# Raw weight bits loaded from ScalarE's queue, chunk outputs queued a step later, the cosine's rounding constant added by ScalarE

## The chip, the cores and the metric

The kernel runs on one core of a Trainium2 chip. The metric is the device time in microseconds of one execution, as the median of three runs. One execution before the change was also recorded by the hardware profiler; all rows below come from that execution.

## The reference, cut to what matters

Three stages follow each other: a linear attention with a norm, a mixture of eight experts with one expert per token, and a dense layer with h * cos(h) between its two products.

```python
kv  = np.einsum('bhsd,bhse->bhde', k, v)            # 8 batches, 8 heads, 576 tokens, 64 wide
out = np.einsum('bhsd,bhde->bhse', q, kv)
x   = out / rms(out) * g_norm                       # -> 4608 tokens x 512

expert_idx = np.argmax(logits(x), axis=1)           # 8 experts, 512 -> 1024 -> 512
y = gate_w * (np.maximum(x @ w1[e], 0) @ w2[e])     # for each token's expert e

h = y @ w_in                                        # 512 -> 2048, w_in is float64
return (h * np.cos(h)) @ w_out                      # 2048 -> 512, w_out is float64
```

## The kernel before, in words

The instructions of each engine run in the order in which the program writes them down, and each engine starts its own instructions and DMAs in that order. An instruction that has to wait for another engine or for a transfer holds up all that stands behind it on its engine. Three engines issue DMAs: SP (`nc.sync`), ACT (`nc.scalar`) and POOL (`nc.gpsimd`), each into its own queue.

**The expert stage** (in the profile some 190 to 720 us) works on 16 chunks of 304 gathered tokens. A loop over `g` runs 130 steps. Step g does for hidden slice f of chunk c the first product (`layer1`, L241 on PE, then the two evictions L247 on ACT and L248 on DVE), and for the slice two steps back the second product (`layer2`, L258). `load_piece` loads the weights of a slice into one of four `raw` tiles by two DMAs on SP (L130, L134), three steps before `split_piece` turns them into high and low parts on ACT (L141) and DVE (L142). `turn_x` transposes the next chunk's tokens (L224, L229, L230) and `gate_x` works out the gate of the next chunk (L182 on POOL to L208 on DVE), writes it to DRAM and reads it back as a broadcast (L212, L216 on SP). When a chunk's last slice is done, `store_y` (L263 to L269) writes the chunk's token list and four output tiles by five DMAs on SP.

**The conversion** of the last layer's float64 weights to float32 is spread over the same steps. The generator `conv` is advanced once or twice at the end of each step. There are 32 conversions: 16 of `w_in` (layer 0), 16 of `w_out` (layer 1). Each loads 512 KB of raw bits into one of two `c_raw` tiles (`convert_load`, `raw_bits`, L283 and L288 on SP), and runs `bits`: an absolute value on ACT into `c_mk` (L297), a multiply and add on POOL (L298), and four integer passes on DVE (L299, L301, L303, L305), with a pause of the generator after the first three. After every second conversion of layer 0, `prepare` adds and splits the blocks and issues seven DMAs of 256 KB on SP (`ws`, L416); a conversion of layer 1 issues one (`wc`, L328). So two conversions of layer 0 take 13 turns of the generator, one of layer 1 takes 4. The load of conversion x + 1 is issued at the start of conversion x: for an even x that is 4 turns ahead of its use, and right behind the seven DMAs of `prepare`; for an odd x it is 9 turns ahead.

**The last stage** (some 720 to 1526 us) runs 72 steps, `step(i)`, eight for each block of 512 tokens. In a step PE makes seven products for h (L1150, 42 matmuls) and then the out-product of step i - 2 (L1243, 24 matmuls). DVE puts the seven products together into two tiles h (L1166). `turns` then forms u = h / (2 pi) on ACT (L1134) and r = u rounded to a whole number on POOL (L1135), by adding and taking away the constant `ROUND` = 1.5 * 2^23. In the next step DVE takes u - r (L1192), ACT the absolute value and the sine (L1170, L1174), DVE multiplies with h (L1175), and ACT and DVE split the result into high and low (`high` L1180, `low` L1184). The tiles u and r have two buffers for the two tiles of a step, so r is written again only after `low` of the step before has read it. Behind `turns`, in steps 1 to 7, `second_split` splits the second weights (L343 on ACT, L344 on DVE), and in the steps in which the next block's tokens are prepared, `tokens_of` does subtractions and splits (L371, L343, L344).

Of the kernel before, what the change touches and what calls it, by code (L numbers as in the profile page):

```python
# [10 lines left out]
F32 = mybir.dt.float32  # L11
F32R = mybir.dt.float32r
I32 = mybir.dt.int32
ACTF = mybir.ActivationFunctionType
ALU = mybir.AluOpType
# [14 lines left out]
CH = 304  # L30
# [6 lines left out]
def tile_kernel(ctx, tc, q, k, v, g_norm, emb, tau, w1, w2, w_in, w_out, out):  # L37
    nc = tc.nc
# [7 lines left out]
    yT = dram.tile([DM, NT + CH], F32, name="yT")  # L46
# [3 lines left out]
    perm = dram.tile([NT + CH], I32, name="perm")  # L50
# [27 lines left out]
    chunks = []  # L78
    for vi, (e, idx) in enumerate(VISITS):
        for i in idx:  # L80
            chunks.append(dict(
                row=(lambda e=e: e * NT + reg(itab[0:1, 0, e:e + 1], CH, mybir.EngineType.Pool)) if i else (lambda e=e: e * NT),
                col=lambda e=e, i=i: reg(itab[0:1, 1 + i, e:e + 1], NT),
# [8 lines left out]
    LAG = 2  # L92
    NC = len(chunks)
# [50 lines left out]
    V = nc.vector  # L144
    P = SimpleNamespace()
# [115 lines left out]
                )  # L261

    def store_y(c):  # L263
        col = c["col"]()
        nc.sync.dma_start(out=perm[bass.ds(col, CH)].rearrange("(p r) -> p r", r=4), in_=c["rows"])
        for d in range(4):
            o = P.yo.tile([128, CH], F32, name="yo", tag="yo")
            V.tensor_tensor(out=o, in0=c["y"][d][:, 0:CH], in1=c["gate"], op=ALU.mult)
            nc.sync.dma_start(out=yT[d * 128:(d + 1) * 128, bass.ds(col, CH)], in_=o)  # L269


    w_in32, w_out32 = w_in.bitcast(I32), w_out.bitcast(I32)
# [5 lines left out]
    CONV = [(0, m) for m in range(DF2 // 128)] + [(1, m) for m in range(DF2 // 128)]  # L278

    def raw_bits(raw, layer, m):  # L280
        rv = raw.rearrange("p c x -> p (c x)")
        if layer == 0:
            nc.sync.dma_start(  # L283
                out=rv.rearrange("p (k c) -> p k c", k=4),
                in_=w_in32[:, m * 256:(m + 1) * 256].rearrange("(k p) c -> p k c", p=128),
            )
        else:
            nc.sync.dma_start(out=rv, in_=w_out32[m * 128:(m + 1) * 128, :])  # L288

    def convert_load(x):  # L290
        cv[x] = P.cv.tile([128, 512, 2], I32, name="c_raw", tag="c_raw", bufs=2)
        raw_bits(cv[x], *CONV[x])

    def bits(raw, t, mk, out):
        lo, hi = raw[:, :, 0], raw[:, :, 1]
        hf = hi.bitcast(F32)
        nc.scalar.activation(out=mk, in_=hf, func=ACTF.Abs)  # L297
        nc.gpsimd.tensor_scalar(out=mk, in0=mk, scalar1=-1.0, scalar2=TINY, op0=ALU.mult, op1=ALU.add)  # L298
        V.tensor_scalar(out=t, in0=hi, scalar1=3, scalar2=0x3FFFFFF8, op0=ALU.logical_shift_left, op1=ALU.bitwise_and)  # L299
        yield  # L300
        V.scalar_tensor_tensor(out=t, in0=lo, scalar=29, in1=t, op0=ALU.logical_shift_right, op1=ALU.bitwise_or)  # L301
        yield
        V.scalar_tensor_tensor(out=t, in0=hi, scalar=-0x40000000, in1=t, op0=ALU.bitwise_and, op1=ALU.bitwise_or)  # L303
        yield
        V.scalar_tensor_tensor(  # L305
            out=out, in0=mk.bitcast(I32), scalar=31, in1=t, op0=ALU.arith_shift_right, op1=ALU.bitwise_and
        )

    def convert(x):
        layer, m = CONV[x]  # L310
        if x == 0:
            convert_load(0)
            yield
        raw = cv.pop(x)
        if x + 1 < len(CONV):
            convert_load(x + 1)
        t = P.cv.tile([128, 512], I32, name="c_t", tag="c_t", bufs=2)
        mk = P.cv.tile([128, 512], F32, name="c_mk", tag="c_mk", bufs=1)
        if layer == 0:
            if m % 2 == 0:  # L320
                cv["a"] = P.sc.tile([128, 1024], F32, name="sa", tag="sa")
            yield from bits(raw, t, mk, cv["a"][:, m % 2 * 512:m % 2 * 512 + 512].bitcast(I32))
            yield
            if m % 2:
                yield from prepare(m // 2, cv.pop("a"))
        else:
            yield from bits(raw, t, mk, t)
            nc.sync.dma_start(out=wc[m], in_=t.bitcast(F32))  # L328
            yield

# [173 lines left out]
    if True:  # L506
# [62 lines left out]
        for i in range(2):  # L569
# [7 lines left out]
            out=ident, in_=ones, pattern=[[1, 128]], compare_op=ALU.is_equal, fill=0.0, base=0, channel_multiplier=-1  # L577
# [322 lines left out]
        for t in range(NTILE):  # L900
            j, b, r = where(t)
# [61 lines left out]
    if True:  # L963
# [43 lines left out]
        for g in range(NC * 8 + LAG):  # L1007
            c, f = divmod(g, 8)
            if g == 8 * NC - 1:
                for _ in prep:  # L1010
                    pass
                nc.scalar.preload_act_table_set("trig_and_small")
            if c < NC:
                if f == 1 and 0 < c < NC - 2:
                    load_list(chunks[c + 2])
                if f == 3 and 0 < c < NC - 2:
                    load_x(chunks[c + 2])
                if f == {0: 0, 1: 2, 2: 0}.get(c):
                    prep = gate_x(chunks[c])
                if f == 7 and 2 <= c < NC - 1:  # L1020
                    for _ in prep:
                        pass
                    prep = gate_x(chunks[c + 1])
                layer1(chunks[c], f)
                if g <= OPEN and ranking:
                    cur["po"] = P.ps_x.tile([128, 512], F32, name="xp", tag="xp").rearrange("p (o x) -> p o x", o=1)
                    for it in ranking:
                        next(it)
                    ranking.clear()
            if c == 1:  # L1030

                for x in {5: (0,), 6: (1, 2), 7: (3,)}.get(f, ()):
                    turn_x(chunks[c + 1], x)
            if g >= LAG:
                c2, f2 = divmod(g - LAG, 8)
                layer2(chunks[c2], f2)
                if f2 == 7:
                    store_y(chunks[c2])
                    if c2 == NC - 2:
                        first["x"] = tokens_of(0, lambda: raw_of()[:, 0:512])  # L1040
            if "x" in first:
                next(first["x"], None)

            if g == 8 * NC - 4:
                assert next(conv, None) is None
                cvctx.close()
                WAB.append(ctx.enter_context(tc.tile_pool(name="wb", bufs=1)).tile([128, 7, 2, 256], F32R, name="wb"))
                weights_again(0)
                weights_again(1)
            if g < OPEN:  # L1050
                paused.clear()
                advance(8)
            splits = bool(late) and late[0][0] <= g
            if splits:
                split_piece(*late.pop(0)[1])
            if g == OPEN - 1:

                for d in range(4):
                    nc.sync.dma_start(out=yT[d * 128:(d + 1) * 128, CH:512], in_=none[:, 0:512 - CH].bitcast(F32))
            if g == OPEN:  # L1060
                assert not ranking
                while active:
                    paused.clear()
                    advance(1)
                after_placing()
                load_list(chunks[2])
                load_x(chunks[2])
            for p in when.get(g, ()):
                late.append((split_at[p], load_piece(p)))
                late.sort(key=lambda x: x[0])  # L1070
            if g >= OPEN:
                for _ in range(1 if splits and g % 3 else 2):
                    next(conv, None)
            if c < NC:
                next(prep, None)
                if c != 1 and c + 1 < NC and 3 <= f < 7:
                    turn_x(chunks[c + 1], f - 3)
# [7 lines left out]
    ROUND = 1.5 * 2.0 ** 23  # L1085
    if True:
# [45 lines left out]

        def turns(p, u, r):
            nc.scalar.activation(out=u, in_=p, func=ACTF.Copy, scale=1.0 / (2 * math.pi))  # L1134
            nc.gpsimd.tensor_scalar(out=r, in0=u, scalar1=ROUND, scalar2=-ROUND, op0=ALU.add, op1=ALU.add)  # L1135

        def times_cos(p, u, r, hi, lo):
            V.tensor_tensor(out=u, in0=u, in1=r, op=ALU.subtract)
            nc.scalar.activation(out=r, in_=u, func=ACTF.Abs)
            nc.scalar.activation(out=u, in_=r, func=ACTF.Sin, scale=-2 * math.pi, bias=half_pi)  # L1140
            V.tensor_tensor(out=r, in0=u, in1=p, op=ALU.mult)
            nc.scalar.activation(out=hi, in_=r, func=ACTF.Copy)
            V.tensor_tensor(out=lo, in0=r, in1=hi.bitcast(F32), op=ALU.subtract)
# [17 lines left out]
        def step(i):  # L1161
# [27 lines left out]
            if prev:  # L1189
                for m in range(2):  # L1190
                    h, u, r, g_ = prev[m]
                    V.tensor_tensor(out=u, in0=u, in1=r, op=ALU.subtract)  # L1192
                cos_a(0)
                cos_b(0)
            if stored is not None:
# [243 lines left out]
```

## Time and profile before

| what | value |
|---|---|
| median of three runs | 1528.04 us (1525.45 to 1530.85) |
| the profiled execution's own time | 1528.09 us |
| its span, first to last instruction | 1526.4 us |
| mean granted TensorE clock | 0.947 of full speed |
| busy in the span: PE, DVE, ACT, POOL | 92%, 70%, 51%, 41% |
| DMA queues of SP, POOL, ACT | 260.46, 19.66, 9.78 MB |

The span is 1.7 us shorter than the execution's own time, which includes what lies around the first and last instruction. Busy shares are means over stages with different limits; a stage is read by its own stretch of the span, and there by which wait ended last.

### The profile page before, as it was taken

The numbers are of one execution on the slowest core, as the hardware profiler recorded it, in microseconds if no ns is written. First come the engines' busy times: TensorE is split into PE (matmuls) and PEld (weight loads), VectorE is DVE, ScalarE is ACT, GpSimd is POOL, SyncE is SP. The second block draws the span as 40 slices with busy tenths as digits, with TensorE's granted clock in tenths as the row PEclk, the third lists the DMA queues.
The fourth block names the chain that finished last, engine by engine and source line by source line (L and its number), as shares of the span: only waits on it lengthen the run. The fifth ranks groups of instructions, "written<-read, shape, count | busy, mean of one in ns | idle before, by whom it ended". The sixth has DMA issues, their size and how long they took to land.

```text
span 1526.4 us, 26934 instructions
## 1 busy us (share of the span) xinstructions
PE 1398.2 (92%) x9545; PEld 1288.3 (84%) x9545; DVE 1066.7 (70%) x2201; ACT 771.0 (51%) x1503; POOL 627.0 (41%) x459
## 2 busy tenths in 40 slices
PE   8877587689889989999889999999999999999996
PEld 8766587679889989999778898988888888888895
DVE  2533865687778688884677777777787777778664
ACT  3534632345345344533555656565656555555553
POOL 0223444353435345540334544444443535354443
PEclk8868788899999999999999999999999999999999
DMA  9999828579667787855856666565665666565550
GB/s 266 258 185 198 241 57 196 147 168 249 190 169 222 206 225 211 201 123 165 279 181 192 215 194 199 181 216 186 201 198 188 207 190 204 169 225 175 178 160 30
DMA packets 223670, 291.71 MB, mean 191 GB/s; under 512 B 33148, under 2 KB 127008, under 8 KB 223528
## 3 DMA queue, kind: packets, MB, share of 16 engines
q1 hardware_dynamic: 202440, 260.46, 59.6%
q0 software_dynamic: 15808, 19.66, 4.8%
q10 hardware_dynamic: 5280, 9.78, 2.3%
q8 instruction: 78, 1.28, 0.4%
q14 instruction: 64, 0.52, 0.1%
HBM read 241.28 MB, written 48.49 MB: 190 GB/s over the span
## 4 chain that ended last, share of the span: by engine, by line
DVE 29%; PE 20%; ACT 20%; issue 10%; DMA 9%; POOL 7%; SPq 2%; another core or an unknown queue 1%; DVEq 0%; ACTq 0%; POOLq 0%
PE hps L241 7%; ACT u L1174 6%; PE y L258 6%; POOL r L1135 5%; ACT r L1170 5%; DVE h L1166 4%; DVE u L1192 4%; DVE one L1166 4%; DMA raw<-in_moe_w 3%; DMA c_raw<-in_moe_w_in 3%; DVE ring L344 2%; DVE g L1184 2%; DVE three L1166 2%; DVE sx L371 2%; PE o L1243 2%
## 5 line engine op out<-in xcount | busy, mean ns | idle before, releaser
L1135 POOL TENSOR_SCALAR r<-u 128x512 f32<-128x512 f32 x144 | 312.8, 2187 | 475.0 <-ACT u L1134 475.0
L1243 PE MATMUL o<-ring,g 128*128 128x512 f32 x1728 | 417.5, 396 | 4.5 <-ACT o_sb L1254 2.1
L1243 PEld LDWEIGHTS o<-ring,g 128*128 128x128 f32 x1728 | 318.8, 188 | 80.9 <-ACT o_sb L1254 4.8
L241 PE MATMUL hps<-xT,ring 128*128 128x304 f32 x1536 | 254.1, 316 | 15.3 <-DVE h L248 6.7
L258 PE MATMUL y<-h,ring 128*128 128x304 f32 x1536 | 242.1, 307 | 10.2 <-ACT ring L141 9.4
L241 PEld LDWEIGHTS hps<-xT,ring 128*128 128x128 f32 x1536 | 230.2, 197 | 18.9 <-DVE h L248 7.9
L258 PEld LDWEIGHTS y<-h,ring 128*128 128x128 f32 x1536 | 226.8, 193 | 11.3 <-ACT ring L141 9.6
L1192 DVE TENSOR_TENSOR u<-u,r 128x512 f32<-128x512 f32 x144 | 117.3, 817 | 104.0 <-POOL r L1135 104.0
L1170 ACT ACTIVATE r<-u 128x512 f32<-128x512 f32 x144 | 90.4, 628 | 190.8 <-DVE u L1192 190.7
L1175 DVE TENSOR_TENSOR r<-u,h 128x512 f32<-128x512 f32 x144 | 99.8, 693 | 53.1 <-ACT u L1174 53.1
L1134 ACT ACTIVATE u<-h 128x512 f32<-128x512 f32 x144 | 91.1, 633 | 81.5 <-DVE h L1166 73.8
L1150 PEld LDWEIGHTS p<-ring,wb 128*128 128x128 f32 x840 | 106.0, 195 | 10.0 <-DVE h L1166 8.6
L142 DVE TENSOR_TENSOR ring<-raw,ring 128x1024 fp32r<-128x1024 f32 x72 | 91.7, 1273 | 31.9 <-ACT ring L141 27.7
L1150 PE MATMUL p<-ring,wb 128*128 128x256 f32 x840 | 107.6, 289 | 6.4 <-DVE h L1166 6.4
L1150 PEld LDWEIGHTS p<-ring,wa 128*128 128x128 f32 x840 | 105.9, 195 | 8.2 <-DVE h L1166 6.7
L1150 PE MATMUL p<-ring,wa 128*128 128x256 f32 x840 | 107.1, 288 | 5.7 <-DVE h L1166 5.7
L247 ACT ACTIVATE h<-hps 128x304 fp32r<-128x304 f32 x128 | 53.4, 417 | 110.3 <-PE hps L241 97.9
L1174 ACT ACTIVATE u<-r,half_pi 128x512 f32<-128x512 f32 x144 | 104.3, 724 | 4.7
L182 POOL TENSOR_TENSOR gx<-xr,g_bc 76x512 f32<-76x512 f32 x64 | 101.7, 1621 | 7.5 <-ACT gx L191 7.5
L165 POOL DMA_INDIRECT xr<-xs,rows x64 | 88.1, 1377 | 39.9 <-issue 15.6
L298 POOL TENSOR_SCALAR c_mk<-c_mk 128x512 f32<-128x512 f32 x32 | 25.2, 788 | 186.1 <-ACT c_mk L297 165.3
L1184 DVE TENSOR_TENSOR g<-r,g 128x512 fp32r<-128x512 f32 x144 | 92.7, 684 | 0.2 <-ACT g L1180 0.2
(230 smaller groups left out, 2054.1 us busy)
## 6 DMA issues: line engine op xcount, KB each, us to landing
wa<-ws SPq DMA_DIRECT2D x252, 256.0 KB
wb<-ws SPq DMA_DIRECT2D x252, 256.0 KB
raw<-in_moe_w SPq DMA_DIRECT2D x144, 256.0 KB
ws<-wa SPq DMA_DIRECT2D x56, 256.0 KB
yT<-yo SPq DMA_DIRECT2D x64, 152.0 KB
xs<-xg ACTq DMA_DIRECT2D x12, 780.0 KB
km<-in_k SPq DMA_DIRECT2D x8, 1024.0 KB
vm<-in_v SPq DMA_DIRECT2D x8, 1024.0 KB
```

Source lines behind the costliest of these rows:

```text
L182: nc.gpsimd.tensor_tensor(out=gx[:, r].rearrange("p (h d) -> p h d", h=H), in0=t[:, r, 0:DM].rearrange("p (h d) -> p h d", h=H), in1=g_bc[ ...
L241: nc.tensor.matmul(out=p[:, 0:CH], lhsT=w[:, a, k * 128:(k + 1) * 128], rhs=c["xT"][b_][k], start=(n == 0), stop=(n == 11),)
L258: nc.tensor.matmul(out=c["y"][d][:, 0:CH], lhsT=w[:, a, 512 + d * 128:512 + (d + 1) * 128], rhs=h[b_], start=(f == 0 and i == 0), stop=(f ...
L1135: nc.gpsimd.tensor_scalar(out=r, in0=u, scalar1=ROUND, scalar2=-ROUND, op0=ALU.add, op1=ALU.add)
L1150: nc.tensor.matmul(out=out, lhsT=w[:, wi, a, k * 128:(k + 1) * 128], rhs=x[xi][:, b_, k * 256:(k + 1) * 256], start=(n == 0), stop=(n == 5),)
L1166: V.tensor_tensor(out=out, in0=x, in1=y, op=ALU.add)
L1170: nc.scalar.activation(out=r, in_=u, func=ACTF.Abs)
L1174: nc.scalar.activation(out=u, in_=r, func=ACTF.Sin, scale=-2 * math.pi, bias=half_pi)
L1175: V.tensor_tensor(out=r, in0=u, in1=h, op=ALU.mult)
L1184: V.tensor_tensor(out=g_[1], in0=r, in1=g_[0].bitcast(F32), op=ALU.subtract)
L1192: V.tensor_tensor(out=u, in0=u, in1=r, op=ALU.subtract)
L1243: nc.tensor.matmul(out=ob[b][t], lhsT=g_[a][:, t * 128:(t + 1) * 128], rhs=w[:, b_, m * 512:m * 512 + 512], start=(q_ == 0 and m == 0 and ...
```

## The change

Raw bits are now started from ACT's queue. Conversion x issues the load of conversion x + 2, into the tile that it has itself just read, one turn after its last DVE pass; the first two loads are issued together at the start, and the first conversion begins one turn later. The `wc` store moves to the turn after the last pass. `store_y` computes the four output tiles where it did, and its five DMAs are issued by `flush` at the end of the next step (for the last two chunks at once). In the last stage ACT makes r = h / (2 pi) + ROUND itself, and DVE takes ROUND off again in the subtraction, which becomes (r - ROUND) - u, of opposite sign; an absolute value follows.

```diff
     def store_y(c):
-        col = c["col"]()
-        nc.sync.dma_start(out=perm[bass.ds(col, CH)].rearrange("(p r) -> p r", r=4), in_=c["rows"])
+        o = [P.yo.tile([128, CH], F32, name="yo", tag="yo") for _ in range(4)]
         for d in range(4):
-            o = P.yo.tile([128, CH], F32, name="yo", tag="yo")
-            V.tensor_tensor(out=o, in0=c["y"][d][:, 0:CH], in1=c["gate"], op=ALU.mult)
-            nc.sync.dma_start(out=yT[d * 128:(d + 1) * 128, bass.ds(col, CH)], in_=o)
+            V.tensor_tensor(out=o[d], in0=c["y"][d][:, 0:CH], in1=c["gate"], op=ALU.mult)
+
+        def flush():
+            col = c["col"]()
+            nc.sync.dma_start(out=perm[bass.ds(col, CH)].rearrange("(p r) -> p r", r=4), in_=c["rows"])
+            for d in range(4):
+                nc.sync.dma_start(out=yT[d * 128:(d + 1) * 128, bass.ds(col, CH)], in_=o[d])
+
+        return flush
...
     def raw_bits(raw, layer, m):
-            nc.sync.dma_start(
+            nc.scalar.dma_start(
                 out=rv.rearrange("p (k c) -> p k c", k=4),
...
-            nc.sync.dma_start(out=rv, in_=w_out32[m * 128:(m + 1) * 128, :])
+            nc.scalar.dma_start(out=rv, in_=w_out32[m * 128:(m + 1) * 128, :])
...
     def convert(x):
         if x == 0:
             convert_load(0)
+            convert_load(1)
+            yield
             yield
         raw = cv.pop(x)
-        if x + 1 < len(CONV):
-            convert_load(x + 1)
...
             yield from bits(raw, t, mk, cv["a"][:, m % 2 * 512:m % 2 * 512 + 512].bitcast(I32))
             yield
+            convert_load(x + 2)
             if m % 2:
                 yield from prepare(m // 2, cv.pop("a"))
         else:
             yield from bits(raw, t, mk, t)
+            yield
             nc.sync.dma_start(out=wc[m], in_=t.bitcast(F32))
-            yield
+            if x + 2 < len(CONV):
+                convert_load(x + 2)
...
                 if f2 == 7:
-                    store_y(chunks[c2])
+                    flush = store_y(chunks[c2])
+                    if c2 >= NC - 2:
+                        flush()
...
                 for _ in range(1 if splits and g % 3 else 2):
                     next(conv, None)
+            if g >= LAG and f2 == 0 and 0 < c2 < NC - 1:
+                flush()
...
         def turns(p, u, r):
             nc.scalar.activation(out=u, in_=p, func=ACTF.Copy, scale=1.0 / (2 * math.pi))
-            nc.gpsimd.tensor_scalar(out=r, in0=u, scalar1=ROUND, scalar2=-ROUND, op0=ALU.add, op1=ALU.add)
+            nc.scalar.activation(out=r, in_=p, func=ACTF.Copy, scale=1.0 / (2 * math.pi), bias=ROUND)
+
+        def parts(u, r):
+            V.scalar_tensor_tensor(out=u, in0=r, scalar=-ROUND, in1=u, op0=ALU.add, op1=ALU.subtract)
 
         def times_cos(p, u, r, hi, lo):
-            V.tensor_tensor(out=u, in0=u, in1=r, op=ALU.subtract)
+            parts(u, r)
...
                 for m in range(2):
                     h, u, r, g_ = prev[m]
-                    V.tensor_tensor(out=u, in0=u, in1=r, op=ALU.subtract)
+                    parts(u, r)
```

## Rows read from the trace of the kernel before

**Rows 1.** Windows by stretch: length, busy us (instructions) by engine, PEclk, DMA share, GB/s.

```profile
290.00:540.00 250.00, 219.61 (x1545) 215.09 (x1544) 185.69 (x360) 111.68 (x246) 104.42 (x80) 0.96 0.77 212
540.00:700.00 160.00, 159.65 (x1171) 159.13 (x1170) 127.11 (x259) 72.26 (x166) 76.50 (x61) 0.99 0.69 174
...
740.00:816.00 76.00, 65.58 (x355) 57.06 (x354) 57.48 (x118) 43.90 (x74) 23.28 (x12) 0.91 0.62 193
816.00:1508.00 692.00, 687.75 (x4245) 611.28 (x4244) 515.82 (x930) 400.94 (x708) 318.42 (x162) 1.00 0.58 188
```

**Rows 2.** Waits of ACT, 290 to 540: waiter <- releaser, total us, times, longest.

```profile
ACT c_mk L297 <- DMA c_raw<-in_moe_w_in: 49.8, 7, 11.4
...
ACT ring L141 <- DMA raw<-in_moe_w: 10.6, 4, 5.8
```

**Rows 3.** Waits of SP's queue, 290 to 540.

```profile
SPq L269 <- DVE yo L268: 48.4, 12, 10.4
```

**Rows 4.** Timeline of PE: start, length, instruction [idle before <-releaser].

```profile
246.71 3.38 PE L258 MATMUL y<-h,ring 128*128 128x304 f32 x12 [9.43 <-ACT ring L141]
...
275.24 0.77 PE L224 MATMUL xp<-ident,xr 76*128 76x76 f32 x4 [7.96 <-DVE xT L230]
...
343.11 0.77 PE L224 MATMUL xp<-ident,xr 76*128 76x76 f32 x4 [4.61 <-DVE xT L230]
...
512.46 3.38 PE L241 MATMUL hps<-xT,ring 128*128 128x304 f32 x12 [3.19 <-DVE h L248]
```

**Rows 5.** Timelines of SP's queue and of ACT in one such step.

```profile
362.88 4.88 SPq L416 DMA_DIRECT2D ws<-wa  x7
...
369.45 1.57 SPq L134 DMA_DIRECT2D raw<-in_moe_w  x1
...
375.76 0.68 ACT L297 ACTIVATE c_mk<-c_raw 128x512 f32<-128x512 f32 x1 [6.88 <-DMA c_raw<-in_moe_w_in]
...
377.25 1.06 ACT L141 ACTIVATE ring<-raw 128x1024 fp32r<-128x1024 f32 x1
```

**Rows 6.** The chain that ended last, one wait of 465 to 475: start, us, what.

```profile
465.67 9.00 DMA raw<-in_moe_w
```

**Rows 7.** Two lines by source: duration ns min/median/max, first and last start.

```profile
L766 ACTq DMA_DIRECT2D xs<-xg x12: 366/367/424, 45.1 to 196.7; - x12
...
L303 DVE SCALAR_TENSOR_TENSOR c_t<-c_raw,c_t x32: 676/693/1783, 249.5 to 659.3; 128x512 int32<-128x512 int32 x32
```

**Rows 8.** Timelines of ACT and DVE, the last stage's first block.

```profile
742.43 1.06 ACT L343 ACTIVATE ring<-ring 128x1024 fp32r<-128x1024 f32 x1 [4.77 <-DMA ring<-wc]
...
763.11 1.36 ACT L1134 ACTIVATE u<-h 128x512 f32<-128x512 f32 x2 [1.01 <-DVE h L1166]
764.37 1.04 ACT L343 ACTIVATE ring<-ring 128x1024 fp32r<-128x1024 f32 x1
...
763.66 1.29 DVE L1184 TENSOR_TENSOR g<-r,g 128x512 fp32r<-128x512 f32 x2
...
768.58 1.28 DVE L1192 TENSOR_TENSOR u<-u,r 128x512 f32<-128x512 f32 x2
```

**Rows 9.** The same two timelines, a step of a later block.

```profile
890.68 1.36 ACT L1134 ACTIVATE u<-h 128x512 f32<-128x512 f32 x2 [1.01 <-DVE h L1166]
...
895.46 0.63 ACT L1170 ACTIVATE r<-u 128x512 f32<-128x512 f32 x1 [3.42 <-DVE u L1192]
...
898.78 1.14 ACT L1180 ACTIVATE g<-r 128x512 fp32r<-128x512 f32 x2
...
894.34 1.09 DVE L1192 TENSOR_TENSOR u<-u,r 128x512 f32<-128x512 f32 x1 [1.82 <-POOL r L1135]
```

**Rows 10.** Waits of PE, 816 to 1508.

```profile
PE o L1243 <- ACT o_sb L1254: 2.1, 5, 0.6
PE p L1150 <- DVE h L1166: 2.1, 6, 0.4
```

**Rows 11.** Timeline of PE, the last out-product.

```profile
1510.14 6.36 PE L1243 MATMUL o<-ring,g 128*128 128x512 f32 x24 [1.53 <-ACT g L1180]
```

## The prediction

> **What bounds the kernel now.** I first cut the span into stretches and read in each how long PE, the engine with the most work, stands idle [rows 1]. Three things are to be seen. From 290 to 540 us, where layer 0's weights are converted beside the expert products, PE is busy 219.61 of 250 us. From 540 to 700, the same products beside layer 1's conversions, it is busy 159.65 of 160: the expert loop can run at PE's pace with conversions beside it. In the last stage PE loses 10.4 us from 740 to 816 and only 4.25 us in the 692 us after that.
>
> So the 90% of the last stage is bound by PE, and what POOL does there is hardly worth anything, though POOL's rounding is often on the chain that ended last: DVE waits 1.82 us for it and ACT 3.42 us behind that [rows 9], while PE is served in time.
>
> Then I asked what could be won from 290 to 540. PE does 1545 instructions there; at the pace of the next stretch (159.65 us for 1171) they take 210.6 us, so at most 39.4 us can go: 30.4 us of idle time and 9.0 us by the clock, whose mean grant is 0.96 against 0.99 [rows 1]. After an idle stretch the first twelve matmuls take 3.38 us [rows 4], where twelve of the same kind need about half.
>
> Last I read who waits. ACT stands 49.8 us, seven times, for raw bits before an absolute value, and 10.6 us for expert weights [rows 2]. Behind the waiting ACT instruction lie the evictions that free PE's accumulators, so ACT's wait is PE's wait, less about a step of buffer. Two of PE's stalls, 4.61 and 3.19 us [rows 4], come behind waits for expert weights; the other 22.6 of the 30.4 us I trace to raw bits. Sharing the 39.4 us in that proportion gives 29.3 us for raw bits and 10.1 us for expert weights.
>
> **The change, part by part.**
>
> *Raw bits.* The late loads are those of the odd conversions: issued 4 turns ahead and behind the seven `ws` DMAs, which take SP 4.88 us to issue [rows 5]. Afterwards every layer 0 load leads by 9 turns, some five steps. I have no load's own duration, but ACT's longest wait for one is 11.4 us [rows 2], and five steps at PE's pace are about 17 us (24 matmuls each, by the 540 to 700 stretch 3.3 us). These waits should vanish. In layer 1 the load keeps its place in the program and only changes queue; PE loses 0.35 us there, so I count nothing. Of the 29.3 us I take 25, since ACT, once released, finds the next late thing sooner. Bounds: all 29.3, or 8, by this step: ACT is released at 375.76 and splits expert weights at 377.25 whose second DMA SP issued at 369.45 [rows 5]; another such load held the chain for 9.00 us [rows 6]. Without the first wait ACT would stand there for most of the same time.
>
> Thirty-two DMA starts are new on ACT. The nearest row is ACT's own store, 0.37 us each [rows 7]: nothing, if it lies beside ACT's computing, or 32 x 0.37 = 11.8 us of ACT. ACT is busy 111.68 of 250 us [rows 1], so I take nothing on the path; without that cover it is 11.8 us. The start also waits for the third DVE pass of its own conversion. Behind it stand the evictions, and PE behind those. Two turns lie between them in the program, so I take 0 here too and keep the case as a rival.
>
> The DMA engines were busy 0.77 of that stretch [rows 1], so they have room; the 25 us rest on the lead of 9 turns and not on the queue. The Trainium skill ("DMA: Bandwidth & Descriptors", section "Issuing engines are not separate DMA queues") speaks against expecting much of a second queue: all issuers share the same sixteen DMA engines, and only issuing time is saved. By that rule alone the raw bits would come hardly sooner and the sum would be that of the third rival below, 1527.5 us; no row here shows both queues busy side by side.
>
> *Chunk outputs.* SP waited 48.4 us, twelve times, for the four products of `store_y` [rows 3], and expert weight loads queued behind. Now the five DMAs, their two address reads included, come a step later, behind that step's weight loads and conversion DMAs, when the tiles are long ready. No reader needs them before the last stage, and the last two chunks keep their place. What is late next on SP are the seven `ws` DMAs, which stay in front of weight loads. So of the 10.1 us I take 3; bounds 0 and all of it. The `wc` store, also one turn later, is counted at nothing, as PE has nothing to lose there.
>
> *Before 290 us.* Two stalls of 9.43 and 7.96 us [rows 4]. The first hangs on the first raw bits, now issued a little earlier; the second ends on DVE, behind work whose order on POOL the change leaves alone, and would take back what the first gives. I take 0, bounds 0 to 5 (half of the first).
>
> *The rounding.* POOL's two operations go; ACT gets two more of 128x512, DVE's subtraction becomes a form with a constant. That form's nearest row has a median of 693 ns [rows 7], the old one 0.64 alone and 1.09 us while POOL worked beside it [rows 8, 9]: no loss. In an ordinary step the path from the sums to the absolute value was u, POOL, DVE, 4.78 us (890.68 to 895.46) [rows 9]. Now it is u, r, u, r on ACT, the first r waiting for DVE's `low`: 1.20 us to that (763.11 to 764.31, worked out below) and three operations at 0.52, 2.8 us. So DVE and ACT win 2.0 us a step. What remains for PE to lose is 4.2 us, half of it behind output copies [rows 10]; I take 3.5 off, bounds 2 and 4.2. At the end PE waits 1.53 us for the last cosine and its 24 matmuls stretch to 6.36 us [rows 11]: 2.3 off, bounds 1 and 3.
>
> In the first block it costs time. There POOL was not the last to finish: DVE's subtraction at 768.58 waits for nothing and follows weight and token splits, and those start with ACT's split at 764.37, right behind u [rows 8]. The new r stands in front of that split. The first r can start when DVE's first `low` has read the old one, 763.66 plus half of 1.29 = 764.31; the second u, the second r and the split follow at 0.52 us each (the pair of 1.14 less one of 0.62) [rows 9]: the split starts at 765.87, 1.5 us later, and all behind it too. Six steps have this form; the seventh hides it behind a transfer of 4.77 us [rows 8]. Two of the six win 0.4 us back because POOL no longer slows DVE. PE waits for DVE here (10.4 us idle), so the sum goes to the end: 4 x 1.5 + 2 x 1.1 = 8.2 us. Bounds: 6.2 with two extra operations at 0.52 only, 11 with no overlap.
>
> **The sum.** 25 + 3 = 28 us off in the expert stage, 8.2 on in the first block, 3.5 and 2.3 off behind it: 25.6 us off the profiled execution's 1528.09 us (span 1526.4 and 1.7 around it), 1502.5 us. Its time equals the median of the runs, 1528.04, so no correction is made. A measurement of this kernel can't tell less than about 0.3% (4.6 us) from no change.
>
> **The rivals.**
>
> *Expert weights take the place of raw bits.* SP still issues seven `ws` DMAs in one go, and weight loads come only three steps ahead, about 10 us, where one held the chain for 9.00 us. For it: rows 5 as read above. Against it: from 540 to 700 PE loses nothing with three-step loads, and SP's 48.4 us are gone. Then 8 + 3 = 11 us go in the expert stage: 1528.1 - 11 + 8.2 - 5.8 = 1519.5.
>
> *All of it goes.* With SP free, both kinds of waits vanish, and the first stalls give 5: 39.4 + 5 off, 6.2 on, 7.2 off: 1482.7. For it: the stretch from 540 on. Against it: the burst of seven is still there.
>
> *The transfers are the limit, and the change does not bring the bits sooner.* Then waits move but stay; with 3 us in the expert stage: 1528.1 - 3 + 8.2 - 5.8 = 1527.5. Against it: the DMA share is 0.77 [rows 1]. The page of the Trainium skill named above ("DMA: Bandwidth & Descriptors") would have this case come true for the queue's move taken by itself.
>
> *Slower: ACT stands at its own DMA starts.* Place: the start of load x + 2 behind DVE's third pass, with the evictions behind it. DVE is busy 185.69 of 250 us [rows 1], and that pass takes up to 1783 ns [rows 7]. With thirty starts, my 25.6 us are gone when each makes PE idle for 0.85 us; at 1.1 us each the time is 1502.5 + 33 = 1535.5. Against it: two turns, about a step, lie between.
>
> **How the numbers follow.** My forecast 0.50, expert weights in place of raw bits 0.20, all of it 0.18, transfers the limit 0.06, slower 0.06. The likeliest is the forecast, 1502.5. The range from 1484 to 1523 leaves out the two last cases, the upper edge of the weight-load case and half of the favourable one, about 2 in 10. Faster by over 0.3% (below 1523.5) is the forecast, the favourable case and most of the weight-load case, 0.85; within 0.3% 0.08; slower 0.07.
>
> **What would show it.** Right: ACT's wait for `c_raw` of layer 0 falls from 49.8 us to a few; PE idles under 10 us in the layer 0 stretch; SP's wait at L269 is gone; PE loses nearly 19 us in the last stage's first block instead of 10.4, where ACT's splits start 1.5 us later behind the sums than now; after that under 1 us. Wrong: ACT waits at L141 as long as it did at L297; or ACT idles in front of its DMA starts; or the first block is not longer, because r was not in the way.

## The result, and the profile after

The changed kernel takes 1486.72 us (median of four runs, 1472.52 to 1489.90) against 1528.13 us for the kernel before on the same chip: a ratio of 0.971 with a 95% interval of 0.964 to 0.978. The forecast was 1502.5 us. The direction was right, the size was not: 41 us were gained where 25.6 were forecast.

The profiled executions, 1528.09 us before and 1489.90 after, are cut at three events on PE: the first expert product, the first of the last stage's seven products, and the end of the span.

| stage, us | before | after | difference | forecast |
|---|---|---|---|---|
| up to the first expert product | 192.1 | 195.8 | +3.7 | 0 |
| expert stage | 527.6 | 490.7 | -36.9 | -28 |
| last stage | 806.8 | 801.1 | -5.7 | +2.4 |
| span | 1526.4 | 1487.7 | -38.7 | -25.6 |

The windows of the kernel after, to be read against [rows 1]. The columns are the same.

```profile
290.00:540.00 250.00, 245.62 (x1819) 244.30 (x1818) 219.40 (x425) 132.92 (x286) 117.11 (x97) 1.00 0.88 236
540.00:690.00 150.00, 149.04 (x1097) 148.10 (x1096) 110.98 (x233) 65.28 (x147) 56.33 (x48) 1.00 0.68 179
800.00:1460.00 660.00, 660.00 (x4125) 591.98 (x4124) 469.64 (x909) 454.32 (x819) 34.89 (x32) 1.00 0.59 194
```

From 290 to 540 us PE does 1819 instructions where it did 1545, at a mean granted clock of 1.00 instead of 0.96, and idles 4.4 us instead of 30.4. The DMA share rises from 0.77 to 0.88: before, there was room. In the last stage PE has no idle time left between 800 and 1460 us, and POOL is nearly out of work.

The waits of ACT and of SP's queue in the kernel after, 290 to 540 us (waiter, releaser, total us, times, longest), against [rows 2, 3]:

```profile
ACT h L247 <- PE hps L241: 57.4, 39, 3.1
...
ACT ring L141 <- DMA raw<-in_moe_w: 4.8, 2, 4.6
ACT c_mk L302 <- DMA raw<-in_moe_w: 4.1, 1, 4.1
```

```profile
SPq L424 <- DVE wa L352: 42.0, 15, 5.2
SPq L212 <- DVE gt L208: 24.9, 9, 5.7
```

ACT's 49.8 us of waits for `c_raw` are gone (at the same instruction, L302, 4.1 us are put down to a weight load, once); most of its waiting is now for PE's products. The wait for expert weights at L141 halved too, from 10.6 to 4.8 us, though nothing in the change names these loads. SP no longer waits for `yo`. It waits 42.0 us for the blocks of `prepare` instead, while PE idles 4.4 us in all.

The first block of the last stage in the kernel after, ACT and then DVE (lines 1146, 1147, 351, 352 and 1199 are 1134, 1135, 343, 344 and 1184 of before), against [rows 8]:

```profile
744.46 0.63 ACT L1146 ACTIVATE u<-h 128x512 f32<-128x512 f32 x1 [1.01 <-DVE h L1181]
745.72 0.63 ACT L1147 ACTIVATE r<-h 128x512 f32<-128x512 f32 x1 [0.64 <-DVE g L1199]
746.26 0.61 ACT L1146 ACTIVATE u<-h 128x512 f32<-128x512 f32 x1
746.78 0.62 ACT L1147 ACTIVATE r<-h 128x512 f32<-128x512 f32 x1
747.30 1.04 ACT L351 ACTIVATE ring<-ring 128x1024 fp32r<-128x1024 f32 x1
```

```profile
745.01 1.28 DVE L1199 TENSOR_TENSOR g<-r,g 128x512 fp32r<-128x512 f32 x2
748.38 1.22 DVE L352 TENSOR_TENSOR ring<-ring 128x1024 fp32r<-128x1024 f32 x1 [2.09 <-ACT ring L351]
```

This is the order that the prediction worked out: the first r 0.71 us into DVE's pair, the split 2.84 us behind the first u (747.30 - 744.46). Before it was 1.26 us (764.37 - 763.11), so the split is 1.58 us later; 1.5 was forecast.

The start of the expert stage brought something that was not foreseen. ACT and PE in the kernel after:

```profile
238.23 5.63 ACTq L288 DMA_DIRECT2D c_raw<-in_moe_w_in  x2
243.97 0.42 ACT L247 ACTIVATE h<-hps 128x304 fp32r<-128x304 f32 x1 [15.32 <-DMA yT<-none]
```

```profile
245.43 3.34 PE L258 MATMUL y<-h,ring 128*128 128x304 f32 x12 [11.41 <-DVE yo L266]
...
279.89 0.77 PE L224 MATMUL xp<-ident,xr 76*128 76x76 f32 x4 [5.52 <-DVE xT L230]
```

ACT stands 15.32 us with evictions behind it. The profile puts this down to the transfer into `yT` that reads the tile `none`. In the program the pool of `none` is closed just before the pool of `c_raw` is opened, so the first two loads probably wait for memory that this transfer still reads; no run here tests that. In the kernel before, the same two loads left SP's queue at 238.80 us, no earlier. Whether ACT's stand costs time is one of the experiments.

### The profile page after: what moved, and what is told of

Its sections match the earlier page's. It is cut to its first block, busy times and chain, and to the rows that moved or that the text cites. A ratio compares the mean times of both kernels' runs of the same rounds, so it can differ in the third digit from the quotient of the medians.

```text
span 1487.7 us, 26770 instructions
## 1 busy us (share of the span) xinstructions
PE 1373.2 (92%) x9545; PEld 1272.5 (86%) x9545; DVE 1032.9 (69%) x2201; ACT 845.8 (57%) x1647; POOL 305.2 (21%) x315
## 5 line engine op out<-in xcount | busy, mean ns | idle before, releaser
L241 PE MATMUL hps<-xT,ring 128*128 128x304 f32 x1536 | 244.2, 308 | 4.5 <-DVE xT L230 3.5
L241 PEld LDWEIGHTS hps<-xT,ring 128*128 128x128 f32 x1536 | 222.6, 191 | 5.8 <-DVE xT L230 4.5
L1270 POOL DMA_INDIRECT out<-o_sb,perm_i x36 | 38.8, 1078 | 799.6 <-ACT o_sb L1269 620.3
L142 DVE TENSOR_TENSOR ring<-raw,ring 128x1024 fp32r<-128x1024 f32 x72 | 98.6, 1369 | 28.7 <-ACT ring L141 23.6
L1147 ACT ACTIVATE r<-h 128x512 f32<-128x512 f32 x144 | 89.8, 624 | 45.2 <-DVE g L1199 45.2
L1150 DVE SCALAR_TENSOR_TENSOR u<-r,u 128x512 f32<-128x512 f32 x144 | 95.7, 688 | 13.3 <-ACT r L1147 10.6
L182 POOL TENSOR_TENSOR gx<-xr,g_bc 76x512 f32<-76x512 f32 x64 | 98.6, 1571 | 4.5 <-ACT gx L191 4.5
L248 DVE SCALAR_TENSOR_TENSOR h<-hps,h 128x304 fp32r<-128x304 f32 x128 | 59.7, 466 | 49.4 <-ACT h L247 44.9
```

Of the source, the lines that this page charges most:

```text
L142: nc.vector.tensor_tensor(out=w[:, 1], in0=raw, in1=w[:, 0].bitcast(F32), op=ALU.subtract)
L182: nc.gpsimd.tensor_tensor(out=gx[:, r].rearrange("p (h d) -> p h d", h=H), in0=t[:, r, 0:DM].rearrange("p (h d) -> p h d", h=H), in1=g_bc[ ...
L241: nc.tensor.matmul(out=p[:, 0:CH], lhsT=w[:, a, k * 128:(k + 1) * 128], rhs=c["xT"][b_][k], start=(n == 0), stop=(n == 11),)
L1147: nc.scalar.activation(out=r, in_=p, func=ACTF.Copy, scale=1.0 / (2 * math.pi), bias=ROUND)
L1150: V.scalar_tensor_tensor(out=u, in0=r, scalar=-ROUND, in1=u, op0=ALU.add, op1=ALU.subtract)
```

## The experiments

**Theory** after the result: the raw bits were late because their loads stood in SP's queue behind instructions that waited, so that anything that takes the loads or the waiting instructions out of that order, or leaves time for it, cures them. **Rivals**: the lead of 4 turns was too short (the prediction's reading), or the transfers themselves were slow (the third rival). Each part of the change was run alone.

**Loads two conversions ahead, from ACT's queue (conv_only), and the same from SP's queue (conv_sp).**

```diff
         if x == 0:
             convert_load(0)
+            convert_load(1)
+            yield
             yield
         raw = cv.pop(x)
-        if x + 1 < len(CONV):
-            convert_load(x + 1)
...
+            convert_load(x + 2)      # after the last pass; conv_only also has nc.scalar in raw_bits
```

> The conversions' part alone: loads two conversions ahead and started by ACT; chunk outputs and rounding as before. Forecast's step: 25 us off in the expert stage and the weight waits stay, about 1503 us. Rival, raw bits were the cause of the weight waits too: the expert stage loses nearly all of its 39 us, about 1489 to 1493 us, and ACT's wait for expert weights from 290 to 540 falls below 3 us with the outputs still queued as before.

> Loads two conversions ahead, but still started by SP, so nothing new stands in ACT's queue. If the lead of 9 turns does it: within 5 us of the run with ACT's queue. If SP's queue does it, because there the loads stand behind chunk outputs, gates and ws: 15 us or more slower than that run, with ACT's wait for layer 0 raw bits above 20 us.

**ACT's queue alone, lead as before (queue_only)**: `nc.sync` becomes `nc.scalar` in `raw_bits`, nothing else.

> Raw bits started by ACT, but one conversion ahead as before. If the lead does it: nearly all of ACT's 49.8 us wait for layer 0 raw bits stays, and the time is within 8 us of before. If the queue does it: the wait falls below 20 us and the time by 20 us or more. By the page's rule on issuing engines, only SP's issuing time is saved: under 5 us.

**Chunk outputs a step later, alone (flush_only)**: `store_y` returns `flush`, as in the diff ahead of the prediction; the raw bits are loaded by SP, one ahead.

> Chunk outputs queued a step later, nothing else. Forecast's step: SP's wait at the yT stores goes, and 0 to 3 us come off. Rival, the outputs held up the raw bits and the expert weights behind them: 10 us or more off, and ACT's wait for raw bits falls by a third or more.

The four ran on one chip, with the kernel before at 1517.00 us:

| kernel | median us | ratio to before (95%) |
|---|---|---|
| conv_only | 1478.75 | 0.974 (0.968 to 0.980) |
| conv_sp | 1479.52 | 0.975 (0.971 to 0.980) |
| queue_only | 1483.96 | 0.979 (0.974 to 0.983) |
| flush_only | 1493.80 | 0.986 (0.981 to 0.990) |

The windows from 290 to 540 us of conv_only, conv_sp, queue_only and flush_only, in this order:

```profile
290.00:540.00 250.00, 247.19 (x1827) 245.70 (x1826) 218.39 (x424) 131.31 (x282) 120.40 (x97) 1.00 0.87 241
```

```profile
290.00:540.00 250.00, 248.07 (x1834) 246.72 (x1833) 222.24 (x425) 132.26 (x285) 123.12 (x97) 1.00 0.86 241
```

```profile
290.00:540.00 250.00, 243.59 (x1776) 240.59 (x1775) 207.92 (x416) 126.04 (x271) 108.97 (x91) 0.99 0.83 234
```

```profile
290.00:540.00 250.00, 243.94 (x1788) 241.59 (x1787) 211.76 (x420) 129.28 (x280) 115.69 (x93) 0.99 0.88 235
```

Every part alone brings PE from 219.6 to between 243.6 and 248.1 us. They are substitutes, not summands: the gains of conv_only and flush_only are 38 and 23 us and would make 61 together, where conv_flush, which has both (below), gains 34. Of the four expectations, the forecast's own step failed in conv_only and flush_only (25 and at most 3 us off). The rivals named there came nearer, but the sign given for conv_only's, ACT's wait for expert weights under 3 us, did not come: it is 6.3 us.

The waits of ACT in queue_only, and then in flush_only, same stretch, with the longest one of flush_only and the load that it waited for, on SP:

```profile
ACT ring L141 <- DMA raw<-in_moe_w: 24.0, 7, 4.8
```

```profile
ACT c_mk L302 <- DMA c_raw<-in_moe_w_in: 13.6, 3, 5.5
ACT ring L141 <- DMA raw<-in_moe_w: 10.3, 5, 3.2
```

```profile
285.33 4.52 SPq L421 DMA_DIRECT2D ws<-wa  x7
290.18 0.59 SPq L288 DMA_DIRECT2D c_raw<-in_moe_w_in  x1
...
298.96 0.69 ACT L302 ACTIVATE c_mk<-c_raw 128x512 f32<-128x512 f32 x1 [5.49 <-DMA c_raw<-in_moe_w_in]
```

In queue_only the lead is still 4 turns for every second load, and no wait for `c_raw` of layer 0 is listed any more; at the same absolute value ACT waits 7.5 us in all, put down to other transfers, so that is the most that can be left. The lead by itself was not too short. In flush_only the loads still stand behind the seven `ws` DMAs of `prepare`, and 36.2 of 49.8 us are gone, so the seven are not the main cause either. But the three waits that are left, 13.6 us, are for loads right behind the seven, which thus have a smaller share. Expert weights make ACT wait more in queue_only than before, 24.0 against 10.6 us, and PE is hardly the worse for it. In conv_sp SP still waits for `yo` (39.6 us, 17 times), and the longer lead covers it. What made the loads late can be seen in SP's queue in another execution of the kernel before (before_again, below), and behind it what ACT waited for:

```profile
370.99 0.32 SPq L265 DMA_DIRECT2D perm<-rows  x1
378.49 2.10 SPq L269 DMA_DIRECT2D yT<-yo  x4
...
381.90 4.65 SPq L416 DMA_DIRECT2D ws<-wa  x7
386.60 0.91 SPq L283 DMA_DIRECT2D c_raw<-in_moe_w_in  x1
```

```profile
395.77 0.67 ACT L297 ACTIVATE c_mk<-c_raw 128x512 f32<-128x512 f32 x1 [8.33 <-DMA c_raw<-in_moe_w_in]
```

SP issues nothing from 371.3 to 378.49, while it stands at the first `yT` store. All later loads slip by these seven microseconds, the raw bits come 9 us after their issue at 386.60, and ACT has been standing for 8.33 us. Not every wait has this form. In the first trace of the kernel before, four of the seven waits in [rows 2] come behind 7.5 to 9.0 us in which SP issues nothing before the `yT` stores, two behind 3.0 and 3.4 us, and the shortest (3.02 us) behind 13.2 us at the gate's store L212.

**The cosine's part alone (cos_only)**: `turns`, `parts` and the two calls of `parts`, as in the diff ahead of the prediction; the expert stage is that of before. With it on one chip ran two repairs of what the changed kernel's profile had shown.

> The kernel before with the cosine's part alone: ScalarE adds the rounding constant, VectorE takes it off; nothing is changed in the expert stage. Theory of the prediction: about 8 us are lost in the last stage's first block (TensorE's idle time there grows from some 13 to some 21 us) and 6 us come back behind it, so the time is 0 to 4 us above the kernel before (ratio 1.000 to 1.003). Rival, from the trace of the changed kernel: its whole last stage, first product to end, was 5.7 us shorter although the first block lost its 8 us, so the part alone is a gain: ratio 0.994 to 0.998.

**The first two raw loads from SP (after_first_sp)**:

```diff
-        raw_bits(cv[x], *CONV[x])
+        raw_bits(cv[x], *CONV[x], eng=nc.sync if x < 2 else None)   # None: nc.scalar
```

> The changed kernel, but the first two raw-bit loads are started by SyncE instead of ScalarE, so ScalarE no longer stands 15.32 us at 243.97 us behind its own DMA starts. Theory A: that stand is a cost of its own; TensorE's stall of 11.41 us at the start of the expert stage goes for the most part and the expert stage becomes 5 to 10 us shorter (480 to 486 us): ratio to the kernel before 0.965 to 0.968. Theory B: the token gathers and the first conversion's long VectorE pass set the start anyway, so that the stall moves behind them: expert stage 488 to 492 us, ratio as for the changed kernel, 0.970 to 0.973.

**POOL rounds in steps 1 to 7 of the last stage (after_pool_first)**:

```diff
+        def turns_pool(p, u, r):
+            nc.scalar.activation(out=u, in_=p, func=ACTF.Copy, scale=1.0 / (2 * math.pi))
+            nc.gpsimd.tensor_scalar(out=r, in0=u, scalar1=ROUND, scalar2=None, op0=ALU.add)
...
-                    turns(h[m], u, r)
+                    (turns_pool if 1 <= i < 8 else turns)(h[m], u, r)
```

> The changed kernel, but in steps 1 to 7 of the last stage GpSimd adds the rounding constant again (one operation, the subtraction stays with VectorE), so that ScalarE's weight split follows straight behind the second u. Theory of the prediction: the 8.3 us that the first block lost came from the r that stands in front of the split; here TensorE's idle time in the first block falls back from 21.9 to about 13.6 us and the last stage takes about 793 us: ratio 0.965 to 0.968. Rival: GpSimd beside VectorE slows the splits by as much, TensorE idles 19 us or more there, and the ratio stays at 0.970 to 0.973.

**Both repairs (after_both)**: the two edits above together.

> The two edits together: the first two raw-bit loads from SyncE, and GpSimd adding the rounding constant in steps 1 to 7 of the last stage. They lie in different stages, so their gains should add, unlike those of the parts in the expert stage: if both theories hold, 12 to 18 us below the changed kernel, ratio 0.959 to 0.963; if only the second holds, 0.965 to 0.968; if neither, 0.970 to 0.973.

Before stood at 1512.25 us on this chip. Measured: cos_only 1511.68 us, ratio 0.9998 (0.9974 to 1.0022); after_first_sp 1477.80, 0.977 (0.973 to 0.981); after_pool_first 1464.85, 0.968 (0.964 to 0.972); after_both 1466.85, 0.971 (0.966 to 0.975).

Taking ACT's stand away wins nothing. ACT and PE in after_first_sp:

```profile
231.98 1.06 ACT L141 ACTIVATE ring<-raw 128x1024 fp32r<-128x1024 f32 x1 [8.34 <-DMA raw<-in_moe_w]
237.10 0.68 ACT L303 ACTIVATE c_mk<-c_raw 128x512 f32<-128x512 f32 x1 [4.07 <-DMA c_raw<-in_moe_w_in]
```

```profile
238.70 3.41 PE L241 MATMUL hps<-xT,ring 128*128 128x304 f32 x12 [7.15 <-DVE h L248]
...
267.63 0.77 PE L224 MATMUL xp<-ident,xr 76*128 76x76 f32 x4 [5.79 <-DVE xT L230]
```

ACT now waits for the weights and the raw bits themselves. PE's stall is 7.15 us (with the stand 11.41, and 7.66 in after_again below), and the next one, 5.79 us, is much the same as with the stand, 5.52. That is theory B's mechanism: the stall moves behind other late things. Neither theory's numbers came: the expert stage took 484.6 us, inside theory A's range, but the changed kernel with the stand takes 482.3 in after_again; and the ratio, 0.977, lies above both ranges. after_both gives no more than after_pool_first: its 0.971 lies above the 0.965 to 0.968 expected if only the second theory holds, with an interval that reaches into that range.

**The changed kernel, and three others, on one chip.** `conv_flush` is the change without the cosine's part, `pool_first_again` repeats after_pool_first, `before_again` is one profiled execution of the kernel before.

> The changed kernel once more, on the same chip as the next three, since chips differ in their times and the start of the expert stage differs between executions. Theory A: the stand of ScalarE behind its first raw-bit starts (15.32 us in the trace shown) belongs to the kernel and comes in this execution too; then the move of these two starts to SyncE would have had to show, and the ratio here is 0.978 or above, as without it. Theory B: the stand is there or not, and the stage loses nothing by it: ratio 0.970 to 0.977.

> The changed kernel without the cosine's part: loads two ahead by ScalarE's queue, and the chunk outputs a step later. The prediction booked 25 and 3 us for the two and 2.4 us of loss for the cosine's part: 2 to 3 us faster than the changed kernel on this chip. By the run of the cosine's part alone (ratio 0.9998) the two take the same time within 0.3%. If the two parts of the expert stage were independent their gains would add to some 60 us (38 and 23 us alone); if they are substitutes, the ratio is that of the loads alone, 0.970 to 0.977.

> GpSimd adding the rounding constant in steps 1 to 7 of the last stage, now on the same chip as the changed kernel. Theory of the prediction (the r in front of the split cost the first block 8.3 us): 6 to 9 us faster than the changed kernel, last stage 793 to 796 us. Rival: its ratio of 0.9682 came from the expert stage's start in those executions, and here it lies within 3 us of the changed kernel.

> The kernel before, for a trace of it on the same chip as the three others: what in the stages is the chip's and what the change's. If the shorter last stage (801 us against 806.8) of the runs with the cosine's part is the change's own, the last stage here is 805 to 808 us; if it is the chip's, 801 to 803 us.

With before at 1511.77 us: after_again 1473.90, ratio 0.974 (0.971 to 0.976); conv_flush 1477.98, 0.975 (0.971 to 0.978); pool_first_again 1463.60, 0.968 (0.964 to 0.972). Their profiled executions, cut as above, and the last stage cut by the starts of its 72 groups of 42 products, one for each step:

| us | first expert product | expert stage | last stage | its first 9 steps | next 62 | rest |
|---|---|---|---|---|---|---|
| before_again | 187.4 | 517.2 | 807.2 | 105.2 | 665.8 | 36.2 |
| conv_flush | 192.3 | 482.9 | 805.5 | 105.2 | 665.4 | 34.9 |
| after_again | 189.9 | 482.3 | 799.8 | 112.6 | 656.0 | 31.2 |
| pool_first_again | 183.3 | 482.8 | 795.4 | 105.8 | 658.0 | 31.6 |

The expert stage gains 34.9 us here and 36.9 on the first chip; conv_flush gains no more than conv_only (0.975 and 0.974). ACT's stand (12.9 us in after_again) is there again, and the ratio of after_again, 0.974, is that of theory B. before_again's last stage, 807.2 us, shows that the shorter one belongs to the change and not to the chip. In the last stage after_again loses 7.4 us against before_again in the first nine steps and wins 9.8 in the next 62 and 5.0 in the rest; against conv_flush, which lacks only the cosine's part, it loses 7.4 and wins 9.4 and 3.7. With POOL rounding in steps 1 to 7 the first nine fall back by 6.8 us. PE in after_again and then in pool_first_again, steps 5 to 7:

```profile
725.88 5.40 PE L1165 MATMUL p<-ring,wb 128*128 128x256 f32 x42 [2.29 <-DVE h L1181]
...
741.71 6.78 PE L1165 MATMUL p<-ring,wa 128*128 128x256 f32 x42 [4.83 <-DVE h L1181]
...
758.70 6.79 PE L1165 MATMUL p<-ring,wb 128*128 128x256 f32 x42 [4.61 <-DVE h L1181]
```

```profile
716.87 5.39 PE L1169 MATMUL p<-ring,wb 128*128 128x256 f32 x42 [1.08 <-DVE h L1185]
...
731.47 6.78 PE L1169 MATMUL p<-ring,wa 128*128 128x256 f32 x42 [3.61 <-DVE h L1185]
...
747.23 6.78 PE L1169 MATMUL p<-ring,wb 128*128 128x256 f32 x42 [3.38 <-DVE h L1185]
```

Each stall is 1.2 us shorter, since ACT's split again follows the u pair directly (719.84 and 721.10 us in pool_first_again, 1.26 us apart as before). This kernel beats both: 48 us below the kernel before, 10 below the changed one. Of the 10, its stages give the edit 4.4 us (799.8 - 795.4); the profiled execution also reached the expert stage 6.6 us earlier, in code that the edit does not touch.

## Why the prediction fell short

**Raw bits and chunk outputs: forecast -28, measured -36.9 and -34.9.** The step that failed is "Of the 29.3 us I take 25, since ACT, once released, finds the next late thing sooner", with "So of the 10.1 us I take 3" for the expert weights. Of the 39.4 us that could go nearly all went. The cause put down for the lateness was wrong ahead of the size: "issued 4 turns ahead and behind the seven `ws` DMAs". queue_only keeps the lead and flush_only keeps the seven, and each removes most of the waits. The loads were late mostly because SP stood at `yT` stores; the seven alone leave 13.6 of the 49.8 us (flush_only). The division of the 39.4 us in the proportion of PE's stalls fails with it: the wait for expert weights was not a second limit that would be met next. It fell to 4.8 us with the whole change, and where it rose, to 24.0 us in queue_only, PE still idled only 6.4 of 250 us. So the first rival (expert weights take the place) had its mechanism in queue_only, but not its price. The second rival, all of it goes, at 1482.7 us, comes nearest to the 1486.7 measured, and in the full change for the reason that it gave: with SP free of the stores both kinds of waits shrink to almost nothing. That its time is so near is partly luck: it books 5 us for the first stalls, which did not shrink (9.43 and 7.96 us before, 11.41 and 5.52 after), and only 1.0 us for the last stage, which gained 5.7. All the signs listed under "Right" came (in the last stage's first block PE idles 8.3 us more than before, 21.9 against 13.6), although the cause was not the one named: none of them told a short lead from a blocked queue.

**The queue.** "The 25 us rest on the lead of 9 turns and not on the queue" failed as well: the queue by itself was worth 33 us (1517.00 to 1483.96). The rule of the Trainium skill ("DMA: Bandwidth & Descriptors", section "Issuing engines are not separate DMA queues"), by which a second issuing engine saves only issuing time, would have given far less: thirty-two starts at 0.484 us, the median of layer 0's sixteen on SP before, are 15.5 us of SP's time by estimate, if all of it were on the path. The seven microseconds at 371 us show why: the saving lay not in transfer rate but in the order, since a load that is ready to go does not stand behind a store that is not. That all issuers share the sixteen DMA engines is not contradicted; the share went from 0.77 to 0.83 in queue_only, so there was room. This ends the third rival.

**ACT's own DMA starts**, the slower rival: 0.375 us each, and the events in front of the sixteen of layer 0 in the kernel after took 38 ns in the median and at most 1.83 us. Counting nothing was right. The first two starts are the exception, 15.32 us; taking them away won nothing, since ACT then waits 8.34 us for the weights and 4.07 us for the raw bits at that place (after_first_sp).

**First block: forecast +8.2, measured +7.4 on both chips** (113.9 against 106.5, 112.6 against 105.2). This is the sum over the first nine steps. For steps 1 to 8, after_again less before_again, it is -1.7, 1.1, 1.6, 1.6, 1.6, 1.7, 1.2 and 0.2: the six steps 2 to 7 sum to 8.8 for the 8.2 forecast, so the mechanism was right. The gain of step 1, in which PE's wait falls from 2.50 to 0.76 us, was not foreseen.

**Later blocks: forecast -3.5, measured -9.9 and -9.8.** The failed step is "What remains for PE to lose is 4.2 us". The column of idle time before an instruction undercounts what a stall costs. PE in before_again, a block's disturbed step (step 46 of the stage, counted from 0), and then the same step in the kernel after:

```profile
1205.90 5.28 PE L1150 MATMUL p<-xb,wa 128*128 128x256 f32 x42
1211.01 5.77 PE L1243 MATMUL o<-ring,g 128*128 128x512 f32 x24
1217.16 5.39 PE L1150 MATMUL p<-xb,wb 128*128 128x256 f32 x42 [0.38 <-DVE h L1166]
```

```profile
1191.78 5.09 PE L1165 MATMUL p<-xb,wa 128*128 128x256 f32 x42
1196.71 5.77 PE L1258 MATMUL o<-ring,g 128*128 128x512 f32 x24
1202.31 5.09 PE L1165 MATMUL p<-xb,wb 128*128 128x256 f32 x42
```

From start to start the disturbed step takes 11.26 us, the undisturbed one 10.53: 0.73 us lost, of which the idle column shows 0.38. The rest is in products that begin 0.17 us before the end shown for those ahead of them when nothing waits, and in a group that takes 5.28 us where 5.09 do; the group of 5.39 us lengthens the next step. In the trace of before, 17 of the 62 steps take 10.82 us or more, together 9.6 us above 10.54, and that sum could have been taken ahead of the change. All 62 against the shortest would give 13.0, too much: many undisturbed steps take 10.62 to 10.65 us, and in the kernel after still 10.62. The Trainium skill ("Perfetto Trace Analysis", section "Tensor Engine Instruction (MATMUL, LD_WEIGHTS)") says that the end of a matmul is an estimate of the profiler and not a measurement; these rows agree, since the next group starts 0.17 us before such an end.

**Tail: forecast -2.3, measured -3.2 and -5.0.** The mechanism was right. In the kernel after, the last three out-products run without a gap, where before the last one waited 1.53 us and was stretched [rows 11]:

```profile
1461.52 16.96 PE L1258 MATMUL o<-ring,g 128*128 128x512 f32 x72
```

**Open.** The part of the cosine wins 5 to 6 us of last stage in two pairs of profiles (806.8 to 801.1 with everything, 805.5 to 799.8 in conv_flush and after_again), but cos_only's time is that of before within 0.24%, 3.6 us, so that neither its theory nor its rival is decided. Its profiled execution has the shorter last stage too, 801.9 us (799.8 to 802.8 in the four profiles with the part as it stands, 803.8 to 807.2 in the seven without), and reached the expert stage at 192.0 us, 4.6 later than before_again. Over fourteen profiled executions that point lies between 183.3 and 195.8 us, in code that none of the edits touches, with and without the cosine's part. Whether cos_only lost its 5 us there by chance is not settled. Nor is why the undisturbed steps take 10.53 and 10.62 us in some executions and 10.58 and 10.65 in others, even of one kernel (after_pool_first and pool_first_again), 2 us over a last stage.

## What to carry to other kernels

When loads are late, look first at what stands in front of them in their own queue and is waiting, not at their lead: here moving the waiting stores back, the loads to another queue, or the loads further ahead were three cures for one illness, and their gains did not add. What ACT's waits for two kinds of loads cost PE was not proportional to their lengths, so a share for each was the wrong way to divide what can be won; the pace of the next, undisturbed stretch was the better forecast. And measure what an engine loses in a periodic stage by the distance of equal steps, the disturbed ones against the undisturbed, not by the sum of its idle times.

## What was not expected of the hardware

DVE's last integer pass of a conversion took 5.43 us while POOL multiplied beside it; the pass before it, of the same form, took 0.68 us. DVE and then POOL in the kernel after, with the same pass beside such products later:

```profile
266.39 0.68 DVE L308 SCALAR_TENSOR_TENSOR c_t<-c_raw,c_t 128x512 int32<-128x512 int32 x1
272.57 5.43 DVE L310 SCALAR_TENSOR_TENSOR sa<-c_mk,c_t 128x512 int32<-128x512 int32 x1 [5.50 <-POOL c_mk L303]
...
398.06 1.60 DVE L310 SCALAR_TENSOR_TENSOR sa<-c_mk,c_t 128x512 int32<-128x512 int32 x1
```

```profile
272.50 4.95 POOL L182 TENSOR_TENSOR gx<-xr,g_bc 76x512 f32<-76x512 f32 x4
...
395.69 6.37 POOL L182 TENSOR_TENSOR gx<-xr,g_bc 76x512 f32<-76x512 f32 x4
```

The pass ends 0.55 us after POOL's four products, and PE's stall of 5.52 us at 279.89 us ends behind it. The Trainium skill ("GPSIMD Engine Reference", section "8. Key points") names contention of GpSimd with VectorE instructions that read two inputs from SBUF; the trace agrees. How long the pass is held differs: in this trace only it and the last pass at 256.96 us (4.18 us) took more than 1.79 us beside such products, and the one at 398.06 took 1.60. What makes the difference is not shown.
